# Batch 0 of a windowed attention + SwiGLU kernel in two token halves, with its first q/k as fp32 on a second queue

## The chip, the cores and the metric

The kernel runs on one core of a Trainium2 chip. The metric is device time in microseconds (us), the median of several executions. The engines are named as in the profile: PE (TensorE, matrix products), PEld (PE's weight loads), DVE (VectorE), ACT (ScalarE), POOL (GpSimd), SP (SyncE, which here only issues transfers). "Span" is the length of the profiled execution; the timed runs are some 2 us above it.

## The reference, cut to what matters

```python
# q, k, v: (4, 8, 768, 64) fp32; 8 global keys, local window of 96
scores = scale * (q @ k.T) + bias         # bias = -slope[head] * distance
keep   = is_global | is_local             # keys 0..7, or 0 <= row - col < 96
a      = softmax(where(keep, scores, -1e9))
x      = (a @ v), heads side by side      # (3072 tokens, 512)
g, val = x @ w_gate, x @ w_val            # (512, 1536) each
out    = (silu(g) * val) @ w_out          # (3072, 512) fp32
```

## The kernel before

Tokens are handled in eight blocks of 384, two to a batch; a block has 12 feed-forward steps (gate, value, and one twelfth of the output products of the block before it). "Step 0.2" is block 0, step 2. Attention of later tokens is slipped between the steps. Before the first step can run, batch 0 needs its attention: this **opening** is what the change is about. Attention goes by pairs of heads.

```python
def load_qk(b, h0, h1):                       # POOL's DMA casts fp32 -> fp16
    for st, src in ((qst[b], q), (kst[b], k)):
        nc.gpsimd.dma_start(out=st[:, h0:h1, :], in_=src[b, h0:h1]...)
def load_globals():                           # the 8 global V rows, all batches
    nc.gpsimd.dma_start(out=vG..., in_=v[:, :, 0:NG, :]...)
    for b in range(B):                        # copied in front of all 7 key chunks
        nc.sync.dma_start(out=vSs[b][0:NG, :, :, :], in_=vG[:, b]...broadcast)
# ... issue order of the opening, all on POOL's queue:
load_qk(0, 0, 2); load_globals(); load_v(0, 0); load_v(0, 1)
for hp in range(1, NP): load_pair(0, hp)      # q, k, V of each pair, whole batch
load_w(0); load_w(1); ...
# ... a pair in the opening: all 768 tokens transposed, two of three score banks
#     (exp on ACT, then a multiplication by a mask on DVE), then half the values
def early(hp, s):
    if s == 0:   pairs[0, hp].transposes()
    elif s < 3:  pairs[0, hp].scores(s - 1, nc.vector)
    else:        pairs[0, hp].values(0, True) # num, den; then xT = num / den on DVE
# ... later score banks, values and batch 1's transposes between steps:
single = [[sc(0, 0, 2)], [sc(0, 1, 2)], [va(0, 0, 1)], ..., [tr(1, 0)], ..., [tr(1, 1)]]
```

The softmax here doesn't subtract the row's maximum and nothing guards it: scores larger than these inputs give would overflow.

## Time and profile before

| | before |
|---|---|
| time, median | 264.18 us (263.57 to 264.3) |
| span | 262.0 us |
| step 0.2 starts / step 0.10 starts | 30.25 / 49.48 |
| PE busy / idle in the span | 240.5 / 21.5 |

The prediction below shows the page's busy rows and slices. One more view: the table by stage, cut at first scores, step 0.2, step 0.10, step 1.0, block 2 and block 7. Columns: stretch; its length; busy time (and number of instructions) of PE, PEld, DVE, ACT, POOL; granted clock (of PE, as a share of full speed); DMA share (packet time over that of 16 engines, which can pass 1); GB/s.

```profile
0.00:8.98 8.98, 1.70 (x24) 1.23 (x26) 2.66 (x12) 3.10 (x4) 7.92 (x15) 1.00 0.95 115
8.98:30.25 21.27, 15.64 (x190) 9.74 (x191) 16.55 (x42) 15.25 (x36) 15.86 (x21) 1.00 1.49 183
30.25:49.48 19.23, 17.24 (x210) 10.22 (x210) 18.21 (x44) 9.45 (x20) 9.09 (x12) 1.00 1.41 198
49.48:54.06 4.58, 4.32 (x36) 2.11 (x33) 3.21 (x9) 4.03 (x10) 0.00 (x0) 1.00 1.61 190
54.06:85.69 31.63, 31.63 (x327) 18.58 (x325) 24.95 (x57) 20.65 (x45) 19.39 (x22) 1.00 0.90 86
85.69:226.97 141.28, 138.70 (x1101) 77.80 (x1100) 109.05 (x242) 66.62 (x141) 56.67 (x63) 1.00 0.64 72
226.97:262.00 35.03, 31.31 (x169) 16.34 (x167) 13.91 (x25) 10.07 (x19) 0.00 (x0) 1.00 0.14 53
```

### The profile page before, as it was taken

The page shows a single profiled execution, that of the slowest core. Times are in us where ns is not written, and L with a number is a line of the kernel's source. Part 1 is how long each engine was busy: PE and PEld are TensorE (multiplying, and loading weights), DVE is VectorE, ACT ScalarE, POOL GpSimd, SP SyncE. Part 2 cuts the span into 40 slices and gives each one's busy share as a digit, 9 for nine tenths or more (in the row PEclk, how much of TensorE's full clock was granted, in tenths as well). Part 3 has the DMA queues.
Part 4 walks back from the last instruction along what each step waited for, and adds up shares of the span by engine and source line. Part 5 has one row for each costly group of instructions (what it writes and reads, how often), then busy time and mean ns, then how long its engine had stood idle before and what let it go on. Part 6 is the DMA issues. An engine that isn't in the chain of part 4 may idle for free.

```text
span 262.0 us, 5362 instructions
## 1 busy us (share of the span) xinstructions
PE 240.5 (92%) x2048; PEld 136.0 (52%) x2048; DVE 188.5 (72%) x429; ACT 129.2 (49%) x273; POOL 108.9 (42%) x130
## 2 busy tenths in 40 slices
PE   1685899799999999999999799999999999999994
PEld 0452456455556645545556455555566555555541
DVE  2499799787986898887768987986668655655610
ACT  3668635587656355552653554463743333332321
POOL 8985643205679884184597810202343100000000
PEclk9999999999999999999999999999999999999999
DMA  8999999976699999487999991110100111101122
GB/s 103 167 169 198 191 205 206 175 84 41 77 94 157 124 110 173 63 53 79 144 150 72 144 127 43 40 39 3 41 33 12 43 40 40 40 3 40 43 80 80
DMA packets 79193, 24.41 MB, mean 93 GB/s; under 512 B 66016, under 2 KB 76096, under 8 KB 79168
## 3 DMA queue, kind: packets, MB, share of 16 engines
q0 software_dynamic: 62368, 14.20, 58.9%
q1 hardware_dynamic: 16800, 9.87, 16.1%
q8 instruction: 16, 0.26, 0.4%
q14 instruction: 9, 0.07, 0.1%
HBM read 28.58 MB, written 6.29 MB: 133 GB/s over the span
## 4 chain that ended last, share of the span: by engine, by line
PE 68%; DMA 15%; DVE 8%; ACT 3%; POOL 3%; issue 2%; DVEq 0%; ACTq 0%; POOLq 0%
PE ops L366 22%; PE vps L339 19%; PE gps L339 19%; DMA kst<-in_k_dram 8%; DMA qst<-in_q_dram 4%; DMA wv<-in_moe_w_val_dram 3%; PE den L288 3%; PE scA L253 2%; PE num L288 2%; DVE sl L352 2%; ACT at L259 2%; POOL vS L117 1%; DVE rb L307 1%; DVE dT L301 1%; POOL qst L112 1%
## 5 line engine op out<-in xcount | busy, mean ns | idle before, releaser
L350 ACT ACTIVATE th<-gps 128x384 f32<-128x384 f32 x96 | 47.7, 497 | 79.5 <-PE gps L339 77.1
L339 PE MATMUL vps<-xT,wv 128*128 128x384 f16 x384 | 78.7, 326 | 2.1 <-DVE sl L352 2.0
L339 PE MATMUL gps<-xT,wg 128*128 128x384 f16 x384 | 78.7, 326 | 1.0 <-DVE xT L314 0.5
L352 DVE SCALAR_TENSOR_TENSOR sl<-th,gps 128x384 f32<-128x384 f32 x96 | 52.5, 547 | 34.6 <-ACT th L350 34.1
L366 PE MATMUL ops<-wo,hT 128*128 128x512 f16 x288 | 76.0, 379 | 0.3
L356 DVE TENSOR_TENSOR hT<-vps,sl 128x384 f16<-128x384 f32 x96 | 52.7, 549 | 7.9 <-PE vps L339 0.6
L311 POOL TENSOR_TENSOR xT<-ns,rb 128x384 f16<-128x384 f32 x24 | 24.1, 1005 | 72.9 <-DVE rb L307 64.6
L339 PEld LDWEIGHTS <-wg 128*128 128x128 f16 x384 | 36.3, 98 | 33.3 <-issue 1.9
L339 PEld LDWEIGHTS <-wv 128*128 128x128 f16 x384 | 36.2, 98 | 28.0 <-issue 5.0
L366 PEld LDWEIGHTS <-hT 128*128 128x128 f16 x288 | 27.2, 98 | 25.2 <-issue 1.3
L259 ACT ACTIVATE at<-scA 128x432 f16<-128x432 f32 x48 | 25.7, 536 | 16.3 <-PE scB L253 16.3
L259 ACT ACTIVATE at<-scB 128x432 f16<-128x432 f32 x48 | 25.9, 540 | 0.0
L123 POOL DMA_DIRECT2D vS<-in_v_dram x24 | 21.2, 888 | 4.4 <-DMA wo<-in_moe_w_out_dram 1.7
L371 ACT ACTIVATE osb<-ops 128x512 f32<-128x512 f32 x24 | 14.5, 604 | 15.1 <-PE ops L366 14.8
L270 DVE TENSOR_TENSOR at<-at,masks 128x432 f16<-128x432 f16 x52 | 18.8, 381 | 4.3 <-ACT at L259 3.9
L288 PE MATMUL den<-at,ones 128*64 128x216 f16 (+6 forms) x288 | 17.8, 235 | 3.6 <-DVE at L270 2.0
L307 DVE STREAM_TRANSPOSE rb<-dR 128x384 f32<-128x384 f32 x32 | 18.3, 573 | 1.7 <-DVE dR L302 0.5
L288 PEld LDWEIGHTS <-ones 128*64 128x64 f16 x288 | 11.7, 111 | 13.3 <-issue 10.3
L301 DVE STREAM_TRANSPOSE dT<-den 128x384 f32<-128x384 f32 x32 | 18.3, 570 | 0.4 <-PE den L288 0.3
L322 ACT COPY ns<-num 128x384 f32<-128x384 f32 x24 | 11.5, 481 | 12.5 <-PE num L288 10.8
L253 PE MATMUL scA<-qT,kT 64*128 64x216 f16 (+2 forms) x112 | 14.8, 251 | 2.7 <-DVE kT L219 2.6
L288 PE MATMUL num<-at,vS 128*64 128x216 f16 (+6 forms) x288 | 14.8, 230 | 0.3 <-DVE xT L314 0.3
(36 smaller groups left out, 175.3 us busy)
## 6 DMA issues: line engine op xcount, KB each, us to landing
out_dram<-osb SPq DMA_DIRECT2D x24, 256.0 KB, 2.0
vS<-in_v_dram POOLq DMA_DIRECT2D x20, 120.0 KB, 6.1
wg<-in_moe_w_gate_dram POOLq DMA_DIRECT2D x4, 384.0 KB, 9.3
wv<-in_moe_w_val_dram POOLq DMA_DIRECT2D x4, 384.0 KB, 10.5
wo<-in_moe_w_out_dram POOLq DMA_DIRECT2D x3, 512.0 KB, 14.1
kst<-in_k_dram POOLq DMA_DIRECT2D x16, 96.0 KB, 3.4
qst<-in_q_dram POOLq DMA_DIRECT2D x16, 96.0 KB, 3.5
qst<-in_q_dram POOLq DMA_DIRECT2D x6, 192.0 KB, 5.9
```

What stands on the lines that cost most here:

```text
L123: nc.gpsimd.dma_start(out=vSs[b][NG:NG + n, c, :, :], in_=v[b, :, KC * c:KC * c + n, :].rearrange("h p d -> p h d"))
L253: nc.tensor.matmul(sc[hi][:, col:col + n], lhsT=self.kT[r, 128 * c:128 * c + 128], rhs=self.qT[r, q0:q0 + n], start=True, stop=True)
L259: nc.scalar.activation(out=at, in_=sc[hi][:, 0:BANK], func=AF.Exp, scale=scale)
L288: nc.tensor.matmul(dst[r, o:o + n], lhsT=ones if ones_side else vSs[b][:, c, 2 * hp + hi, :], rhs=self.at[hi, cb][:, col:col + n], start=( ...
L301: nc.vector.transpose(dT[:, 0:n_q], den[:, 0:n_q])
L307: nc.vector.transpose(rb[:, 0:n_q].rearrange("p (n i) -> p n i", i=32), dR[:, 0:nb].unsqueeze(2).broadcast_to([128, nb, 32]))
L311: nc.gpsimd.tensor_mul(dst, ns[:, 0:n_q], rb[:, 0:n_q])
L339: nc.tensor.matmul(gv[f, which][:, 0:TB], lhsT=w[:, c, 128 * f:128 * f + 128], rhs=xT[:, c, TB * t:TB * t + TB], start=(c == 0), stop=(c = ...
L350: nc.scalar.activation(out=th, in_=dst[:, 0:TB], func=AF.Tanh, scale=0.5)
L352: nc.vector.scalar_tensor_tensor(out=sl, in0=th, scalar=1.0, in1=dst[:, 0:TB], op0=AluOp.add, op1=AluOp.mult)
L356: nc.vector.tensor_mul(hTs[t][:, f, :], dst[:, 0:TB], gv["sl"])
L366: nc.tensor.matmul(ops, lhsT=hTs[t][:, f, 128 * i:128 * i + 128], rhs=wo[:, f, :], start=(f == 0), stop=(f == NFF - 1))
```

## The change

The intent: start the feed-forward steps sooner. Batch 0 is cut in two halves of 384 tokens. Only half 0 is done in the opening. Its q/k come as fp32 through SP's queue, which is free, and are cast on DVE and ACT. V comes in chunks of 120 keys. In the opening, and for part of half 1, the distance bias is added by PE (a product of a diagonal matrix with the distances) before the exponential, in place of DVE's mask multiplication. Half 1's attention moves between steps 2 and 9. Steps 0.10 to 1.2 run without output products, which block 1 then makes up ("deferred"). Twelve plus three dummy matmuls are meant to bring PE's clock up.

The diff, cut to its core (smaller changes, such as one mask multiplication for both heads of a pair, are left out):

```diff
+    for hp in range(NP):                      # half 0, fp32, SP's queue
+        for st, src in ((k32, k), (q32, q)):
+            nc.sync.dma_start(out=st[:, 2 * hp:2 * hp + 2, :],
+                in_=src[0, 2 * hp:2 * hp + 2, 0:TB, :].rearrange(
+                    "h (p j) d -> p h (j d)", p=128))
...
-    def load_v(b, h): ...
+    def load_v_first(h0, h1):
+        for c in range(4):
+            n = min(KC, TB - KC * c)
+            nc.gpsimd.dma_start(
+                out=(vS3 if c == 3 else vSs[0][:, c])[NG:NG + n, h0:h1, :],
+                in_=v[0, h0:h1, KC * c:KC * c + n, :].rearrange("h p d -> p h d"))
...
-    WF = 384
+    WF = 256                                  # 6 pairs of weight pieces, not 4
...
+        def bias(self, half, which):          # slopeI = -slope/scale * identity
+            sc = banks("sc")
+            for hi in range(2):
+                for col, d0, n in BIAS[half, which]:
+                    nc.tensor.matmul(sc[hi][:, col:col + n],
+                        lhsT=slopeI[:, 2 * self.hp + hi, :], rhs=dist[:, d0:d0 + n],
+                        start=(col == 0), stop=False, skip_group_check=True)
+            return sc
...
+    load_globals()
+    copy_globals(0)                           # SP, behind the eight q/k loads
+    load_v_first(0, 4)
+    load_v_first(4, 8)
...
+    fill(12)
+    p_cast(0, V, A); p_bias(0); p_tr(0, V); p_cast(1, V, A); fill(3); p_sc(0)
+    p_tr(1, V); p_cast(2, V, A); p_bias(1); p_sc(1)
+    load_w(0); load_w(1); load_w(2)
+    p_va(0); p_tr(2, V); run_later(9); p_cast(3, V, A)
+    load_half(k16[:, 1], k, 1, 0, H); load_half(q16[:, 1], q, 1, 0, H)
+    for c in range(3, NCH): load_v_rest(0, c)
+    load_w(3)
+    for b in range(1, B): copy_globals(b)     # SP
...
+    stretches = [
+        (ff(0, 0, 10), half1),
+        (ff(0, 10, 12) + ff(1, 0, 3), []),    # bare: no output products
+        (ff(1, 3, 12, (1, 1, 2)), fst), ...
```

## The prediction

> **What bounds the kernel now.** I read the page from the top: busy times, then the 40 slices.
>
> ```profile
> PE 240.5 (92%) x2048; PEld 136.0 (52%) x2048; DVE 188.5 (72%) x429; ACT 129.2 (49%) x273; POOL 108.9 (42%) x130
> ...
> PE   1685899799999999999999799999999999999994
> ...
> DVE  2499799787986898887768987986668655655610
> ...
> DMA  8999999976699999487999991110100111101122
> ```
>
> TensorE (PE) has the most work, and a slice is 6.55 us: from the eighth slice on PE is nearly always busy, while in the first seven it is not, and there VectorE (DVE) and the DMA engines stand at 7 to 9. So the kernel has an opening of some 50 us that PE does not set, and then a long stretch that PE does. I cut it at the feed-forward steps, which the timeline shows (block 0 step 2 at 30.25, step 10 at 49.48, block 2 at 85.69):
>
> ```profile
> 0.00:5.79 5.79, 0.00 (x0) 0.00 (x0) 1.38 (x9) 2.30 (x3) 4.74 (x10) 1.00 0.69 102
> 5.79:28.76 22.97, 16.13 (x205) 10.46 (x205) 17.28 (x44) 14.91 (x34) 17.61 (x25) 1.00 1.49 175
> 28.76:49.48 20.72, 18.45 (x220) 10.73 (x220) 18.76 (x45) 10.58 (x22) 10.52 (x13) 1.00 1.40 198
> 49.48:85.69 36.21, 35.95 (x361) 20.68 (x358) 28.16 (x65) 24.68 (x54) 19.39 (x22) 1.00 0.99 99
> 85.69:203.60 117.91, 115.33 (x969) 64.88 (x968) 95.58 (x218) 58.94 (x126) 55.84 (x63) 1.00 0.74 80
> ```
>
> Columns: length, then busy time of PE, its weight loads, DVE, ScalarE (ACT) and GpSimd (POOL), clock, DMA share, GB/s. In 28.76:49.48 DVE is busy 18.8 of 20.7 us: that stretch is DVE's. What ends the opening is also DVE's, the last pair's normalisation:
>
> ```profile
> 28.14 0.56 DVE L314 TENSOR_TENSOR xT<-num,rb 128x384 f16<-128x384 f32 x1
> ...
> 28.76 0.32 PE L339 MATMUL gps<-xT,wg 128*128 128x384 f16 x1 [0.53 <-DVE xT L314]
> ```
>
> The bracket says that PE stood still until DVE had written xT. The waits add two transfers, the first q and batch 1's q:
>
> ```profile
> PE trq L204 <- DMA qst<-in_q_dram: 6.9, 2, 5.8
> PE scA L253 <- DVE kT L219: 2.6, 4, 1.4
> PE den L288 <- DVE at L270: 2.0, 2, 1.0
> ```
>
> Two traps. Overlapping matmuls hide short waits, so I count work instead: in the undisturbed end a feed-forward step (gate, value, a twelfth of the output products) starts every 1.95 us, 0.65 for each of the three. And DVE durations overlap:
>
> ```profile
> 38.27 0.54 DVE L352 SCALAR_TENSOR_TENSOR sl<-th,gps 128x384 f32<-128x384 f32 x1
> 38.73 0.57 DVE L301 STREAM_TRANSPOSE dT<-den 128x384 f32<-128x384 f32 x1
> 39.34 0.23 DVE L302 RECIPROCAL dR<-dT 128x12 f32<-128x12 f32 x1
> 39.48 0.49 DVE L356 TENSOR_TENSOR hT<-vps,sl 128x384 f16<-128x384 f32 x1
> 39.89 0.56 DVE L307 STREAM_TRANSPOSE rb<-dR 128x384 f32<-128x384 f32 x1
> 40.38 0.51 DVE L352 SCALAR_TENSOR_TENSOR sl<-th,gps 128x384 f32<-128x384 f32 x1
> ```
>
> From start to start, sl and hT cost 0.46 and 0.41 to 0.46, so 0.92 a step; a normalisation (dT, dR, rb, xT) costs about 1.8.
>
> **What the Trainium skill says.** "DMA: Bandwidth & Descriptors", section SWDGE vs HWDGE vs iDMA: only GpSimd's DMAs cast. So q/k from the SP queue must land as fp32 and be cast on an engine, as the change does. Its part on issuing engines adds that all queues share the same 16 DMA engines, so a second queue saves only issue time. The trace agrees with the premise: POOL spends 0.7 to 0.9 us on each issue and is busy 17.6 of 23 us in the opening. "TensorE: Matmul & The Clock Gate", Part 1: PE runs at half rate until busy for about 3.4 us. The trace fits: twelve transposes took 0.85 at 5.79 and 0.53 at 19.00. That is what the added dummy matmuls are for. "SBUF — State Buffer", two separate sides: a two-port DVE copy locks GpSimd out of writing descriptors; the new casts are such copies, and no row before shows the cost.
>
> **The change, part by part.**
>
> *First data.* POOL's first q landed at 5.75, k at 6.70. SP issues cost about 0.4 each; the constants (162 KB) landed 2.5 us after issue. Constants, k0, q0 issued at 0.7, 1.1, 1.5 should land by about 4.3. Cast (estimate 0.3 on DVE, 0.5 on ACT), six transposes each, half-width copies (half of 0.9 and 0.8): first scores near 6.4, against 8.98.
>
> *Pairs 0 to 3.* Before, 4.6 to 4.8 us a pair. DVE per pair now: kT copies and globals 0.95, cast 0.3, normalisation 1.8 = 3.05; the two mask products (0.67 + 0.80) are gone. ACT: exps of 432, 432, 168, 168 at about 1.35, qT 0.45, cast 0.45 = 2.25. PE pays 1728 columns of bias a pair over both halves at 0.65/1536 us each, 0.73 us, or 2.9 us in all. Walking the order of instructions with these costs, scores start at 6.4, 8.8, 11.3, 15.35; the last denominators come at 17.5 and the last xT at 20.4 (28.7 before). Block 0 step 2 starts at 22.2, against 30.25: **8 us earlier**.
>
> *But half 1 moves behind it.* Its transposes and kT copies, formerly in the opening, now lie in steps 2 to 9. DVE there, from 21.0: ten steps x 0.92 = 9.2, and per pair kT copies 0.7, one mask 0.55, normalisation 1.8, x4 = 12.2; sum 21.4, so 42.4. PE: eight steps x 1.3 + 7.7 of attention = 18.1, ending at 40.3. DVE is again the bound; with 1 us of unevenness, 43.4. **This gives back about 2 us**: the same point was 49.48 before, less 1.4 for batch 1's first transposes, already done there.
>
> *Transfers.* Saturated, a weight transfer (786 KB read) lands every 1.95 us, 400 GB/s. Half of q/k (1.57 MB), V (0.8) and constants land by about 9.8, the six first weight pieces by 17.6, second q/k halves by 21.5 (needed at 22.2: tight), batch 1's first q/k by about 44, against 49. The 1.6 us of PE waiting for it at 47 to 49.5 should vanish.
>
> *Deferred output products.* No work is removed. Steps 10, 11 and block 1's 0 to 2 run bare: 5 x 1.3 = 6.5, to 49.9. The rest of block 1: nine steps x 1.3, twelve output parts x 0.65, attention 7.8 (four transposes 0.7, score pairs 0.57, values 0.67) = 27.3. Before, by the same count, 3.9 us of 36.2 were lost here; DVE and ACT at some 70% should lose 2. Block 2 starts at 79.2 against 85.69: **6.5 us**.
>
> *After that* the two are nearly the same. Before lost only about 1.7 us in 85.69:203.60 by this count; merged masks and earlier key spreading may save 0.5. Span 262.0 - 6.5 - 0.5 = 255.0; timed runs are about 2.1 above the span, so 257.1. A schedule this finely set has probably been tuned further than my walk allows for, so I take 256.5.
>
> **Rivals.** (1) *DVE swallows the gain*: steps 2 to 9 become so crowded (ACT about 17.6 of 21 us, gate banks three instead of four) that they end at 47 instead of 43.4. For it: DVE's 18.8 of 20.7 already. Then 260 to 261. (2) *Transfers bind*: q/k, V and weights share the same engines, and 256-byte V rows and 1 KB weight rows are small; casts may starve descriptors. V for pair 0 or the second q/k half late by 2 to 3 us gives 259. Against: saturated rows show 400 GB/s, and the opening was limited by issue. (3) *The deferral pays more*: PE work without DVE work now fills block 1, the stalls there and later go to nearly none, and the opening closes at 20: 251 to 253.
>
> **Range and chances.** Faster by 2% means below 258.9. My sum is 2 us under that with an error of perhaps 3.5: 0.75 faster, 0.23 same, 0.02 slower. Slower needs more than 5 us of new stalls, against 8 saved at the start. Range 251 to 261.
>
> **What would show it.** First scores at 6 to 7; last xT of the opening near 20.4; step 2 near 22; DVE at 90% or more until 42 to 44; no PE wait for batch 1's q; block 2 near 79; from there to the end 176 us, as before. The prediction is wrong if step 2 starts after 25, if step 10 starts after 46, or if the part after block 2 changes by over 3 us.

## The result, and the profile after

The changed kernel took **264.91 us** (median of four runs, 264.61 to 265.39), against 263.94 for four runs of the kernel before beside it (the 264.18 above is the median of three of these). The ratio is 1.0038, with a 95% interval of 1.0014 to 1.0063: the same within 2%, and if anything slower. (A ratio here is the mean time of one kernel's fast runs over that of the other's fast runs of the same rounds, so it is not quite the ratio of the medians.)

The busy times and four rows of the slices (6.56 us each) of the changed kernel's page:

```profile
PE 247.5 (94%) x2119; PEld 140.5 (54%) x2119; DVE 183.1 (70%) x420; ACT 134.4 (51%) x295; POOL 102.1 (39%) x119
...
PE   6677999899999999899999999999999999999994
...
PEclk9959999999999999999999999999999999999999
DMA  7999999990146999990158996991011101101122
```

PE's share rose from 92 to 94% of a span that did not shrink: idle time fell by 6.4 us (21.5 to 15.0) and busy time rose by 6.9. By groups of PE's instructions, with overlapping time counted once, the new busy time is 4.9 us of bias products and 3.5 us of dummy matmuls; the rest (transposes, value products, all else) sums to 1.4 less. The clock row shows one slice, the third (13 to 20 us), at half: PE had stood still just before. But the row, and the clock column of the tables by stage, read full speed also where the trace holds no clock record, and here the first record is at 9.80 us. Before it the matmuls' own times say half. The same eight score products:

```profile
7.78 0.68 PE L325 MATMUL sc<-qT,kT 64*128 64x216 f16 x8
20.59 0.43 PE L325 MATMUL sc<-qT,kT 64*128 64x216 f16 x8
```

So by records and times together PE ran at full rate from 9.80 to 13.21 and from 20.04 on; in the kernel before, from 17.32 on.

The table by stage, cut at the same events but for one (step 0.10 at 47.93; then step 1.3, where output products begin again, at 55.92, in place of step 1.0):

```profile
0.00:7.78 7.78, 5.43 (x34) 3.21 (x35) 5.00 (x27) 2.27 (x3) 6.62 (x13) 1.00 0.87 165
7.78:27.15 19.37, 14.28 (x167) 9.74 (x167) 10.02 (x27) 11.16 (x30) 12.12 (x16) 0.82 1.68 190
27.15:47.93 20.78, 20.20 (x251) 11.66 (x248) 17.81 (x45) 15.47 (x40) 10.86 (x14) 1.00 1.43 198
47.93:55.92 7.99, 7.05 (x45) 3.89 (x41) 7.18 (x16) 4.02 (x10) 0.23 (x1) 1.00 1.60 171
55.92:83.75 27.83, 27.83 (x302) 16.14 (x300) 21.17 (x47) 20.02 (x43) 6.53 (x8) 1.00 0.28 34
83.75:227.09 143.34, 141.22 (x1165) 79.58 (x1164) 107.93 (x237) 71.37 (x151) 64.93 (x70) 1.00 0.86 84
227.09:262.50 35.41, 31.47 (x169) 16.32 (x167) 14.01 (x26) 10.06 (x19) 0.83 (x1) 1.00 0.14 52
```

Three things can be read off. Step 0.2 starts at 27.15, 3.1 us earlier than before, not 8. In steps 2 to 9 PE is busy 20.20 of 20.78 us, DVE only 17.81: PE is the fuller engine there, not DVE. And the part after step 0.10 takes 214.6 us, 2.1 *more* than before (262.0 - 49.48 = 212.5).

What held up the opening is in the timeline of PE. In brackets: the idle time before an instruction, and what the profile holds responsible.

```profile
10.36 0.44 PE L325 MATMUL sc<-qT,kT 64*128 64x216 f16 x8
10.72 0.45 PE L396 MATMUL den<-at,ones 128*64 128x216 f16 x8
14.35 0.57 PE L396 MATMUL num<-at,vS 128*64 128x216 f16 x4 [3.18 <-DMA wg<-in_moe_w_gate_dram]
```

The denominators of pair 0 are done at 11.2, the numerators start at 14.35. The name in the bracket is misleading: a numerator does not need a weight of the feed-forward part. The semaphore it waits for is the one of SP's copy of the global V rows. That copy was issued at 7.21, behind SP's eight q/k loads, and the last of its completions came at 14.21. The Trainium skill, "DMA: Bandwidth & Descriptors", section "Why a DMA increments its semaphore by 16 and not by 1", says how to read this: on the hardware queue only the engines that the transfer uses report, one by one, after a first jump, and only the full count means that all has landed. The trace agrees: one jump at 8.49, then eight single updates from 12.28 to 14.21.

The landing times of the trace tell the rest of the opening. "Predicted" are the numbers of the prediction.

| landed (us) | predicted | after |
|---|---|---|
| first q (the first scores need it: predicted 6.4, measured 7.78) | 4.3 | 5.97 |
| V of half 0, last chunk (heads 0-3 / 4-7) | 9.8 | 11.95 / 13.96 |
| sixth weight piece | 17.6 | 24.04 |
| second q/k halves | 21.5 | 26.08 and 28.14 |

The six weight pieces themselves came 1.3 us apart at the end, as the prediction's rate says. But V was 4 us late, and the first weight piece landed only 3 us after V, while SP's copies of the global rows for batches 1 to 3 were running (their last updates: 16.56, 17.91, 18.99).

The longest waits of PE in the changed kernel (total, number, longest):

```profile
PE num L396 <- DMA wg<-in_moe_w_gate_dram: 3.2, 1, 3.2
PE vps L467 <- DVE sl L480: 1.6, 4, 0.7
PE gvps L467 <- DVE xT L424: 1.2, 1, 1.2
...
PE trs L278 <- ACT q L533: 1.2, 1, 1.2
```

The wait for batch 1's q (1.1 of the 6.9 us in the first line of the prediction's list; the other 5.8 are the first q of all) is gone, as predicted, though not for the reason given (see below).

### The profile page after: what moved, and what is told of

It is laid out like the page before. It is cut to its first block, busy times and chain, and to the rows that moved or that the text cites. A ratio compares the mean times of both kernels' runs of the same rounds, so it can differ in the third digit from the quotient of the medians.

```text
span 262.5 us, 5522 instructions
## 1 busy us (share of the span) xinstructions
PE 247.5 (94%) x2119; PEld 140.5 (54%) x2119; DVE 183.1 (70%) x420; ACT 134.4 (51%) x295; POOL 102.1 (39%) x119
## 3 DMA queue, kind: packets, MB, share of 16 engines
q1 hardware_dynamic: 18848, 11.45, 20.2%
## 4 chain that ended last, share of the span: by engine, by line
PE 69%; DVE 16%; ACT 4%; issue 4%; POOL 3%; DMA 2%; POOLq 0%; DVEq 0%; ACTq 0%
PE ops L496 20%; PE vps L467 19%; PE gps L467 18%; PE nd L396 6%; PE sc L348 3%; DVE rb L417 3%; DVE sl L480 3%; DVE dT L412 3%; DMA wg<-in_moe_w_gate_dram 2%; DVE hT L484 2%; POOL vS L154 2%; ACT at L357 2%; DVE xT L424 1%; DVE dR L413 1%; PE trs L252 1%
## 5 line engine op out<-in xcount | busy, mean ns | idle before, releaser
L467 PE MATMUL vps<-xT,wv 128*128 128x384 f16 x376 | 76.7, 326 | 2.0 <-DVE sl L480 1.6
L467 PE MATMUL gps<-xT,wg 128*128 128x384 f16 x376 | 77.0, 327 | 1.3 <-DVE hT L484 0.8
L357 ACT ACTIVATE at<-sc 128x432 f16<-128x432 f32 x72 | 33.0, 538 | 3.7 <-PE sc L348 3.7
L409 ACT COPY ns<-nd 128x384 f32<-128x384 f32 x28 | 13.4, 478 | 17.2 <-PE nd L396 16.4
L417 DVE STREAM_TRANSPOSE rb<-dR 128x384 f32<-128x384 f32 x32 | 18.1, 568 | 0.9
L368 DVE TENSOR_TENSOR at<-at,masks 128x864 f16<-128x864 f16 x20 | 14.4, 721 | 3.4 <-ACT at L357 3.2
L412 DVE STREAM_TRANSPOSE dT<-nd 128x384 f32<-128x384 f32 x28 | 16.1, 573 | 0.3 <-PE nd L396 0.3
L396 PEld LDWEIGHTS <-ones 128*64 128x64 f16 x288 | 11.2, 111 | 7.9 <-issue 7.1
L333 ACT ACTIVATE at<-sc 128x432 f16<-128x432 f32 (+2 forms) x32 | 11.9, 443 | 3.5 <-PE sc L325 3.5
L186 POOL DMA_DIRECT2D kst<-in_k_dram x16 | 13.7, 871 | 0.0
L186 POOL DMA_DIRECT2D qst<-in_q_dram x16 | 13.6, 862 | 0.0
L396 PE MATMUL nd<-at,ones 128*64 128x216 f16 (+6 forms) x256 | 13.2, 231 | 0.0
```

Of the source, the lines that this page charges most:

```text
L186: nc.gpsimd.dma_start(out=st[:, h // 2, :, h % 2, :], in_=src[b, h].rearrange("(t p) d -> p t d", p=128))
L357: nc.scalar.activation(out=at[:, hi, :], in_=sc[hi][:, 0:BANK], func=AF.Exp, scale=scale)
L396: nc.tensor.matmul(dst[r, o:o + n], lhsT=ones[:, 0:64] if ones_side else vals[:, 2 * hp + hi, :], rhs=self.at[cb][:, hi, col:col + n], sta ...
L412: nc.vector.transpose(dT, den[:, 0:TB])
L417: nc.vector.transpose(rb.rearrange("p (n i) -> p n i", i=32), dR.unsqueeze(2).broadcast_to([128, TB // 32, 32]))
L467: nc.tensor.matmul(gv[f, which][:, 0:TB], lhsT=w[:, c, 128 * f:128 * f + 128], rhs=x_of(t)[:, c, :], start=(c == 0), stop=(c == NC - 1))
```

## The experiments

All are edits of the changed kernel, except e8. Each row gives the time, the kernel before in the same rounds, and the ratio; then, from the profiled run, where steps 0.2 and 0.10 start, the span, and "rest" = span less the start of step 0.10. The kernel before falls into two groups in the same rounds, 263.2 to 265.0 and 265.4 to 266.6, and the ratios average over both: against the lower group alone they would be 0.001 to 0.003 higher. The trace of each kernel is of one run. Two kernels, e2 and e12, compute something else.

| run | us | before | ratio (95%) | 0.2 | 0.10 | span | rest |
|---|---|---|---|---|---|---|---|
| before | 263.94 | | | 30.25 | 49.48 | 262.0 | 212.5 |
| after | 264.91 | 263.94 | 1.0038 (1.0014-1.0063) | 27.15 | 47.93 | 262.5 | 214.6 |
| e1 | 269.72 | 264.03 | 1.0208 (1.0168-1.0247) | 24.45 | 52.80 | 267.5 | 214.7 |
| e2 | 265.38 | 264.03 | 1.0046 (1.0008-1.0085) | 28.82 | 49.05 | 263.8 | 214.8 |
| e3 | 264.73 | 264.03 | 1.0012 (0.9952-1.0072) | 27.47 | 48.89 | 263.4 | 214.5 |
| e4 | 268.81 | 264.03 | 1.0164 (1.0121-1.0207) | 25.68 | 52.21 | 266.8 | 214.6 |
| e5 | 264.67 | 264.46 | 0.9999 (0.9953-1.0045) | 27.09 | 47.75 | 262.6 | 214.9 |
| e6 | 265.75 | 264.46 | 1.0044 (1.0000-1.0088) | 27.81 | 48.77 | 263.7 | 214.9 |
| e7 | 265.41 | 264.46 | 1.0026 (0.9981-1.0070) | 27.74 | 48.40 | 263.3 | 214.9 |
| e8 (before, edited) | 264.95 | 264.46 | 1.0006 (0.9952-1.0060) | 30.32 | 48.74 | 263.9 | 215.2 |
| e9 | 267.49 | 264.23 | 1.0103 (1.0051-1.0156) | 25.30 | 50.39 | 265.4 | 215.0 |
| e10 | 263.30 | 264.23 | 0.9960 (0.9922-0.9999) | 24.92 | 46.30 | 261.2 | 214.9 |
| e11 | 264.46 | 264.35 | 0.9987 (0.9939-1.0036) | 24.55 | 46.68 | 262.5 | 215.8 |
| e12 | 262.00 | 264.35 | 0.9903 (0.9865-0.9941) | 23.34 | 45.64 | 260.3 | 214.7 |
| e13 | 262.63 | 264.15 | 0.9920 (0.9878-0.9963) | 24.65 | 45.30 | 260.2 | 214.9 |
| e14 | 262.96 | 264.15 | 0.9936 (0.9888-0.9984) | 24.74 | 44.95 | 260.7 | 215.8 |

The last column already says something: whatever is done to the opening, the rest of the changed kernel takes 214.5 to 215.8 us. The time is decided by when step 0.10 starts.

**Theory A**: the opening and steps 2 to 9 are set by the sum and the order of the transfers, which share the same DMA engines. **Rivals**: PE's new bias products ate the gain; the deferral cost time; DVE is full and gives back whatever the opening gains.

### e1: the first global rows loaded directly

```diff
-    load_globals(); copy_globals(0)
     load_v_first(0, 4)
+    first_globals()   # four POOL loads: v[0, :, 0:8] into chunks 0, 1, 2 and the cut one
     load_v_first(4, 8)
+    load_globals(); copy_globals(0)      # SP's copy, now for chunks 3 and up only
```

> The changed kernel's PE stands still 3.2 us (11.2 to 14.35) before its first num product. Theory A: what it waits for is not a weight load, as the wait row says, but the copy of the 8 global V rows, which sits on the SP queue behind the eight fp32 q/k loads and lands at 14.21. With these rows loaded straight from DRAM by GpSimd (four loads of 64 rows), num should start near 12 to 12.5, the half-rate clock after the stall should go, and block 0 step 2 should start at 24 to 25 instead of 27.15. The end then moves by 2 to 3 us to about 262 us if nothing later absorbs it. Rival B: the second q/k halves (landing 26.1 and 28.1) and the crowded steps 2 to 9 absorb it: step 10 stays within 1 us of 47.9 and the time stays at 264 to 265.

Step 0.2 came 2.7 us earlier, at 24.45, so the copy had held it up. But the kernel got slower by 4.8 us. Its longest waits of PE:

```profile
PE trs L281 <- DMA k<-in_k_dram: 2.9, 1, 2.9
PE trs L281 <- DMA q<-in_q_dram: 2.4, 1, 2.4
```

The second q/k halves landed at 28.07 and 30.81. SP's copies now ran while the weights came, and these landed 2.4 to 2.7 us apart in place of 1.3 (17.49, 19.88, 22.62, 25.21). The Trainium skill, "DMA: Bandwidth & Descriptors", section "Queues, rings and completion order", has each DMA engine take turns between the queues that have work for it. The landing times fit that: a small copy on one queue slowed large loads on the other. A wait was taken away and a longer one came in its place. The clock added to it: by its records PE was at half rate from 29.08 to 35.90, after these waits, and its busy time between steps 0.2 and 0.10 was 22.53 us in place of 20.20.

### e2: no bias products (wrong)

```diff
-            for hi in range(2):
-                for col, d0, n in BIAS[half, which]: nc.tensor.matmul(...)
...
-                        rhs=self.qT[r, q0:q0 + n], start=not biased, stop=True,
+                        rhs=self.qT[r, q0:q0 + n], start=True, stop=True,
```

> Wrong on purpose: the bias products of batch 0 (40 matmuls) are left out and nothing replaces them. Theory A (waits for transfers and DVE set the opening): step 2 moves by less than 0.5 us, since PE is idle there anyway; steps 2 to 9 get shorter by 4 x 0.3 = 1.2 us of PE work; the time falls by about 1 us, to 264. Rival C (PE work added by the change is what ate the gain): the whole estimate of 2.9 us comes back, 262 us.

All 40 bias products are gone, the relative error is 0.45, and the time is 265.38, which neither theory had. Steps 2 to 10 became 0.55 us shorter (20.23), and step 0.2 came 1.7 us later. Of that, 1.1 are SP's copy of the global rows, which landed at 15.32 in place of 14.21. And PE stayed at half rate until 25.70 (eight score products still took 0.68 at 21.90). So leaving the bias out did not bring the gain back; but as the clock changed with it, e2 does not show what the bias costs in the opening by itself.

### e3: no deferral

```diff
-        (ff(0, 10, 12) + ff(1, 0, 3), []),
-        (ff(1, 3, 12, (1, 1, 2)), fst),
+        (ff(0, 10, 12), []),
+        (ff(1, 0, 12, (1,)), fst),
```

> The output products of block 0 are not put off: block 1 has one part per step and attention of batch 1 from its step 0. My prediction gave the bare steps a use. Theory A: the deferral moves PE work without removing any and gains nothing by itself, but it gives the loads of batch 1's q/k (landing 48.9 to 54.7) time: without it PE waits for them at about 51 and the time is 1 to 2 us longer, 266 to 267. Rival D: the five bare steps (8.0 us measured for 6.5 of PE work) are themselves a loss that the deferral causes; without it the time falls by 1 us or more, to 263 to 264.

From step 0.10 to block 2 it takes 35.99 us against 35.82 with the deferral, and the rest 214.5 against 214.6. Both A and D missed: the deferral is worth nothing and costs nothing that these runs could show.

### e4: first q/k halves through POOL, as fp16

```diff
-        for st, src in ((k32, k), (q32, q)): nc.sync.dma_start(...)      # and no casts
+    load_first(0); load_globals(); copy_globals(0); load_first(1)         # POOL, casting
+    load_v_first(0, 4); load_first(2); load_first(3); load_v_first(4, 8)
```

> The fp32 SP loads and the casts are undone: q/k of batch 0's first half come as fp16 from GpSimd, in token halves as in the changed kernel, pairs 0 and 1 ahead of V. Theory A (all loads share the same engines and their sum sets the opening): the first scores come within 1 us of 7.8 and step 2 within 1.5 us of 27.15, and the time is 264 to 266. Rival E (the SP queue is what brought the first data forward): first scores at 9 to 10, step 2 at 29 or later, time 266 to 268.

This undoes the second queue. The first scores start *earlier* than with it, at 6.21 against 7.78, which neither A nor E had, and so does step 0.2 (25.68 against 27.15). So the queue of its own did not bring the first data forward. Step 0.2 is not the queue's work alone, though: with SP free, the copy of the global rows was issued at 6.02 and landed at 9.66, not at 14.21. Then the second halves land at 27.59 and 29.69, PE waits 1.1 and 1.7 us for them, runs at half rate from 29.03 to 35.86, and the kernel is 1.6% slower than the one before. It is e1's pattern again.

### e5, e6, e7: the copies late, V whole, the halves first

```diff
 # e5: copies for batches 1 to 3 by POOL, at steps 0.9 and 1.2, not by SP in the opening
-    for b in range(1, B): copy_globals(b)
+    at_step(0, 9, ..., lambda: copy_globals(1))
+    at_step(1, 2, lambda: copy_globals(2), lambda: copy_globals(3))
 # e6: e5, and first_globals() as in e1, but behind V of all heads
+    load_v_first(0, 8); first_globals(); load_globals()
 # e7: e6, and the third pair of weight pieces behind the second q/k halves
-    load_w(2)
     load_half(k16[:, 1], k, 1, 0, H); load_half(q16[:, 1], q, 1, 0, H)
+    load_w(2)
```

> One thing alone: the copies of the global V rows of batches 1 to 3 leave the SP queue (where they run at 12 to 19 us) and go to GpSimd behind batch 1's q/k. Batch 0's copy stays. In the run with direct globals the weight pieces landed 2.4 to 2.7 us apart while these copies ran and 1.3 us apart before and after. Theory A (the sum of what must land before the second q/k half sets the opening, and these small copies are a costly part of it): the second q half lands 2 to 3 us before 28.14, with step 2 still near 27 because batch 0's copy is unchanged, steps 2 to 4 keep near 4.8, the time 263 to 265. Rival F (the copies ride along for nothing, the weight loads were slow for another reason): the second q half stays at 27.5 to 28.5.

The weights now land 1.3 to 1.6 us apart from 15.02 on, and the second halves 2 us earlier, at 24.02 and 26.17: SP's copies had cost that. But PE still waits for batch 0's copy (2.0 us) and step 0.2 does not move (27.09), so the earlier halves are worth nothing.

> Both mended: copies late, batch 0's first global rows straight from DRAM, V of the first half in 4 loads of all heads instead of 8, so that GpSimd issues less. Theory A: num of pair 0 starts at about 12 to 13, step 2 at 24 to 25 as in the run with direct globals, and the second q half lands at 25 to 26, so that steps 2 to 4 wait about 1 us, not 5; step 10 at 45 to 46, the time 261.5 to 263.5. Rival B (steps 2 to 9 absorb): step 10 at 47 or later, time 264.

> As the last, and the second q/k halves are loaded ahead of the third pair of weight pieces, which is needed two steps later. Theory A: the second q half lands 2.6 us earlier (23 or before), step 2 at 24 to 25 and no wait for it, step 4 by 30, step 10 at 44 to 45.5, the time 260.5 to 262.5, faster than both kernels. Rival B: step 10 at 47 or later, time 264, since DVE and PE need 20 us for steps 2 to 9 with queues between them however early they start.

Both missed. The global rows now came behind V of all heads and landed, for the first chunk, at 14.45 and 14.20. By its semaphores pair 0's first numerator waited for these, and PE stood for 2.7 and 3.1 us: step 0.2 at 27.8 and 27.7. (In e6 and e7 alike the profile names another load.) In e9 below the same rows, loaded between the two parts of V, landed at 11.46. So what pair 0 needs must not stand behind V of the other heads. In part it may be chance: in e6, 15 of the 16 completions of V's third chunk were in at 11.89, the last only at 13.89.

### e8: the same for the kernel before

```diff
 # before: copies for batches 1 to 3 by POOL, behind load_qk(1, 2, 4) and V of batch 1
-        for b in range(B): nc.sync.dma_start(out=vSs[b][0:NG], ...)
+        copy_globals(0, nc.sync)
...
+    copy_globals(1, nc.gpsimd); ...; copy_globals(2, nc.gpsimd); copy_globals(3, nc.gpsimd)
```

> The kernel before with the same one mend: copies of batches 1 to 3 out of the opening. If the copies cost the transfers 1.3 us each as theory A has it, the third and fourth pairs' q/k there land 2 to 4 us earlier (they landed at 15.3 and 18.9), but DVE at 4.6 us a pair was as much its bound: the last xT comes 0 to 2 us before 28.7, the time is 262 to 264. Rival F: nothing moves.

Pairs 2 and 3 had their k at 14.06 and 17.61 in place of 15.26 and 18.92, and step 0.2 came at 30.32 as ever. The opening of the kernel before is not set by these transfers. Step 0.10 did come 0.7 us earlier, but then PE waited 2.0 us for batch 1's q and k of the third pair, which landed at 56.00 and 57.96 in place of 54.21 and 56.15. "Copies late" is not a gain in itself.

### e9 and e10: e1 and e5 together; then the halves first

```diff
 # e9: order of e1, copies late as in e5 (batch 0's behind load_w(3))
+    load_v_first(0, 4); first_globals(); load_v_first(4, 8); load_globals()
 # e10: e9, and load_w(2) behind the second q/k halves
```

> Wrong theory or right: e1 (global rows of the first chunks loaded directly, between the V loads of heads 0-3 and 4-7) brought step 2 forward to 24.45 but its other copies, still on SP, slowed the weights and the second q/k halves (28.07/30.81). Here the order of e1 is kept and all copies that are not needed in the opening are issued late by GpSimd, as in e5. Theory A (the opening is a sum and order of transfers: each of e1 and e5 took away one of two limits, only both together pay): step 2 at 24.2-25, second q/k halves landed by 24.0 and 26.2, wait of PE for them under 0.5, steps 2 to 10 in 20.5-21.5, step 10 at 45.0-46.3, the rest 214.7, span 259.7-261, time 262-263.3, ratio to before 0.990-0.995. Rival B (the gain is eaten by VectorE and PE in steps 2-9 whenever the opening ends earlier): steps 2 to 10 in 23 or more with no wait for q or k, time 264.5 or more. Rival C (the second halves cannot land before 26 whatever): PE waits 1-2 for them, step 10 at 47, time 264.

> As e9, with the third pair of weight pieces moved behind the second q/k halves, which so need to wait for four pieces and not six. Theory A: the second halves land 2.6 earlier than in e9 (about 21.5 and 23.6), the third pair of weight pieces at about 24.5 and 26, needed only by step 4 at about 29; so no wait for q or k at all, step 10 at 44.8-46, time 262-263.2: as e9 or up to 0.5 less. Rival C (it is the halves that bind in e9): clearly less than e9, by 0.5-1.5. Rival B: as e9, at 264.5 or more.

e9 missed: the weights landed 1.3 to 1.7 us apart from 17.45 on, so the halves came at 26.81 and 29.07, and PE waited 0.7 us for k and 1.9 for q. Rival C came nearest. Its clock was at half too, from 30.36 to 33.77 (PE busy 21.86 us between steps 0.2 and 0.10). e10, which only swaps two pairs of transfers, took these waits away: step 0.2 at 24.92, 0.10 at 46.30, and 263.30 us. Here three edits stand together, the direct rows, the late copies and the halves ahead (not every pair of them was run), and the last swap alone is worth 4.2 us between e9 and e10, waits and clock together.

### e11 and e12: what still sets the two parts?

```diff
 # e11: e10, half 1's first scores masked by DVE again, not biased by PE
-            p.scores_half(1, which, banks("sc") if which else p.bias(1, 0), not which)
+            p.scores_half(1, which, banks("sc"), False)
 # e12: e10, q/k of pairs 2 and 3 not loaded (casts read pairs 0 and 1): wrong on purpose
-    for hp in range(NP):
+    for hp in range(2):
```

> What sets steps 2 to 9 (21.4 from step 2 to step 10 in e10)? This is e10 with the first scores of half 1 masked by VectorE multiplications again (two for each pair, some 0.5 a pair) in place of TensorE's bias matmuls (16 in all, some 1.6). Theory A (TensorE is the bound there: 20.2 of 20.8 busy in the changed kernel, VectorE 17.8): steps 2 to 10 in 19.6-20.6, step 10 about 1 earlier than in e10, the rest unchanged at 214.7, time 262.0-262.8. The prediction's view (VectorE is the bound): steps 2 to 10 in 22.5 or more, time 264.3 or more. Rival C (neither, a chain through both): within 0.4 of e10.

> Wrong on purpose: e10 with the first q/k halves of pairs 2 and 3 not loaded at all (their casts read pairs 0 and 1 again), which takes 0.79 MB out of the opening and no instruction of any engine but four issues on SP. Theory A (the bytes moved set the opening): V, weights and second q/k halves land some 2 earlier, step 2 at 22.5-23.3 instead of 24.9, steps 2 to 10 as in e10, time 261-262. Rival (a chain of casts, copies, exps and normalisations of four pairs sets the opening by now): step 2 at 24.4-25, time 263 as e10.

e12: without 0.79 MB of the opening's reads, step 0.2 comes 1.6 us earlier (23.34). Bytes count there, for most of the 2.0 that they would take at the rate of the weight pieces (524 KB in 1.33 us), an estimate. (The clock differs too: e12 is at full rate from 10.27 on, e10 is at half from 8.07 to 14.89.) (Its output passed the tolerance, though about an eighth of all tokens has wrong scores in half of its heads.) But step 0.10 gains only 0.7: from 0.2 to 0.10 it now takes 22.30. e11 took 22.13 there, and decided nothing, because PE waited 0.7 us for q and 0.9 for a copy of global rows that I had put too late.

### e13 and e14: those waits taken away

```diff
 # e13: e10 with
-    load_half(k16[:, 1], k, 1, 0, H); load_half(q16[:, 1], q, 1, 0, H)
-    load_w(2)
+    load_half(k16[:, 1, 0:4], k, 1, 0, 4); load_half(q16[:, 1, 0:4], q, 1, 0, 4)
+    load_w(2); copy_globals(0)           # no longer behind load_w(3)
+    load_half(k16[:, 1, 4:], k, 1, 4, H); load_half(q16[:, 1, 4:], q, 1, 4, H)
 # e14: e13, and half 1's first scores masked by DVE as in e11
```

> This is e10 with two late transfers mended: the second q/k halves of heads 0 to 3 go alone ahead of the third pair of weight pieces (their q lands about 2 earlier, near 23.7), those of heads 4 to 7 behind it, and the copy of batch 0's global rows for the later chunks is issued before these (it landed at 34.8 and TensorE waited 0.5 for it). Theory A (in e9 to e12 the stretch from step 2 to 10 grew above 20.8 only by waits for transfers): step 2 at 24.5-25, steps 2 to 10 in 20.5-20.9, step 10 at 45.2-45.8, rest 214.8, span 260.2-260.7, time 262.2-262.9. Rival (VectorE takes it back): steps 2 to 10 stay at 21.3 or more with no wait for a transfer, time 263.3 or more.

> e13 with e11's masks: half 1's first scores masked by VectorE, not by TensorE's bias products. Without the waits for transfers that e11 had (0.7 and 0.9), the stretch from step 2 to 10 tells which engine sets it. TensorE sets it: 16 matmuls (0.39 a pair, 1.6) less, so about 1 less than e13, 19.5-20, time 0.8 less than e13. VectorE sets it: VectorE has 1.1 more work (19.0 against 17.8), so 0.5 or more longer than e13. A chain through both: within 0.3 of e13.

The tables by stage, cut at steps 0.2, 0.10 and 1.3; first e13:

```profile
0.00:24.65 24.65, 17.94 (x200) 11.61 (x201) 14.50 (x54) 13.45 (x33) 19.02 (x30) 1.00 1.23 165
24.65:45.30 20.65, 20.07 (x249) 11.62 (x247) 17.80 (x45) 15.45 (x40) 12.88 (x18) 1.00 1.53 194
45.30:53.30 8.00, 7.05 (x45) 3.90 (x42) 7.19 (x16) 4.03 (x10) 2.99 (x4) 1.00 1.30 203
```

then e14:

```profile
24.74:44.95 20.21, 19.40 (x235) 10.52 (x232) 18.87 (x51) 15.39 (x40) 12.20 (x17) 1.00 1.53 194
44.95:53.42 8.47, 7.04 (x44) 3.90 (x41) 7.63 (x17) 4.03 (x10) 3.31 (x4) 1.00 1.31 204
```

e13 did what theory A said: steps 2 to 10 are back to 20.65, and between 24 and 46 us only one wait of PE of over 0.2 us is left (0.6, for a kT copy of DVE). At 262.63 us it **beats both kernels**, the one before by 0.8% (0.9920, interval 0.9878 to 0.9963; by 0.5% against its lower group, and each of e13's six runs is below each of the 11 beside it). The changed kernel was not run in these rounds. So the 0.7 us that e10 lost between steps 2 and 10 came from late transfers, and DVE took nothing back; what e11 and e12 lost beyond that was not tested apart.

e14 then moves 0.7 us of busy time from PE and puts 1.1 on DVE. Steps 2 to 10 get *shorter*, by 0.44, not longer: DVE is not the bound there, though the prediction said so. But the gain is smaller than the work removed, and the bare steps after it get longer by 0.47 (PE's wait for DVE's sl there grows from 0.7 to 1.2), so it is gone at step 1.3. None of the three expected cases came as stated: PE weighs more than DVE in steps 2 to 9, but DVE is close behind.

One rival was not in the list: the clock. The changed kernel was at half rate from 13.21 to 20.04, e13 from 9.66 on at full rate. But e14, at half from 11.06 to 17.88, starts step 0.2 only 0.1 later than e13. So the clock is not what e13 gained in the opening.

## Why the prediction was wrong

The working came to a span of 255.0; it was 262.5. By its own steps:

| step of the sum | predicted | measured | error |
|---|---|---|---|
| step 0.2 starts | 22.2 | 27.15 | +4.95 |
| steps 0.2 to 0.10 | 21.2 | 20.78 | -0.4 |
| step 0.10 to the end | 211.6 | 214.6 | +3.0 |

The other 0.9 us to the 256.5 are the 0.6 that I took off without a reason from a view, and 0.3 between the span of the profiled run and the median. Of the three signs that the prediction named for being wrong, two came: step 2 after 25 and step 10 after 46. The part after block 2 changed by 2.4, less than its 3.

**Failed: "should land by about 4.3" and "landed by about 9.8".** The rate of 400 GB/s was read from weight transfers in a saturated stretch. From 3.79 to 13.96, worked out from the sizes, some 2.2 MB of q, k and V were read, 220 GB/s. The walk through the opening then took PE's, DVE's and ACT's durations and let V be there. Rival (2) named the case ("V for pair 0 or the second q/k half late by 2 to 3 us gives 259"), but I counted only one of the two, and did not see the copies of the global rows in the diff: they moved behind eight loads on the queue that the change had filled. A better order, with the first global rows loaded directly, recovers 2.5 of the 4.95 (e13 against the changed kernel, step 0.2 at 24.65). Of the 2.45 left, bytes are a part (e12), and the chain of casts, copies and normalisations is presumably the other; the runs do not divide it.

**Failed: "from there to the end 176 us, as before".** I compared the start of block 2 in both, but not how much attention was done by then. Counted from the trace: before had 440 attention matmuls left at that point, the changed kernel has 504. The part after block 2 took 178.75 us against 176.31, and PE's busy time in it rose by 2.7. So the predicted "6.5 us" at block 2 was not like for like. What the kernel really had in hand at step 0.10 was 1.55 us, and of that 1.4 were two pairs of batch 1's transposes that it had not yet done.

**Failed: the deferral.** "3.9 us of 36.2 were lost here" was set against the profile's own row, which the prediction shows: PE 35.95 busy of 36.21. Most of the 3.9 was work that my count had left out (the 64 matmuls). e3 measured the deferral at nothing. The bare steps took 8.0, not 6.5, and the rest of block 1 took 27.8, not 29.3: the two errors cancel.

**Half right: "DVE is again the bound" and "gives back about 2 us".** The length was right (21.2 against 20.78). The reason was not: DVE was busy 17.8 us of it, where the walk summed 21.4 from start to start; PE was busy 20.2, where the walk had 18.1. The views said so before: the prediction's row 28.76:49.48 has PE at 18.45 beside DVE's 18.76, and of the seven slices in which it calls PE not busy, the sixth and seventh (33 to 46 us) show PE at 9. e14 agrees: more work for DVE did not lengthen these steps.

**Right, but by luck**: PE no longer waits for batch 1's q. The reason was wrong: its first q and k were to land by about 44 and landed at 50.84 and 48.91, no earlier than the ones waited for before (47.91 and 48.98); PE no longer waits because the first transposes moved to 57.31. **Right**: the casts cost about what was said (ACT 0.51 to 0.55, DVE 0.35 to 0.63); whether they held up POOL's descriptors, as rival (2) feared, no run shows apart. Bias was sized at 2.9 and measured at 4.9 (4.2 in e13, which had more of it at full clock), but without it, in e2, the time did not fall.

A plain budget would have warned of this. PE was busy for 240.5 us before. With the 2.9 of bias that the prediction counted and the dummies (3.5 as measured) it is 246.9, which leaves 8.1 us of idle time in a span of 255.0. Outside the opening the kernel before already idled 8.6, and only 2.0 of that, between steps 0.2 and 0.10, lay where the change could reach it. So the prediction asked for an opening that idles 1.5 us or little more. The changed kernel's idles 7.4, e13's 6.7.

## What to carry to other kernels

Before trusting a walk through the instructions, subtract: the span you predict, less the bounding engine's work, is the idle time that you claim will be left; see in which rows it could be. When an opening waits for data, list every transfer with its size and its place on its queue, small copies too, and ask of each which instruction needs it; moving one limit alone (e1, e4, e5) gave a new wait or nothing, and so did two (e9); taking away all that bound paid. And compare two schedules only at points where the same work has been done.

## What the Trainium skill lacked or had wrong

- "DMA: Bandwidth & Descriptors", "Queues, rings and completion order": it says that engines take turns between queues, but not what a small transfer on one queue costs large ones on the other. Here: weight pieces landed 2.4 to 2.7 us apart while SP's copies of the global rows ran (e1), and 1.3 to 1.7 apart in the same order without them (e9); in e5 two late q/k loads came 2 us earlier once these copies were moved.
- "DMA: Bandwidth & Descriptors", "Issuing engine by pattern": it calls the hardware queue generally faster, and has no figure for a load that needs a cast as well. Here (fp32 in DRAM, needed as fp16) the first scores came at 6.21 with POOL's casting loads (e4) and at 7.78 with SP's fp32 loads and casts; the order of the loads differed as well, so no run shows the queue alone.
- "TensorE: Matmul & The Clock Gate", Part 1: its table has the clock fall to half after at least one idle window of about 3.4 us. (Elsewhere the page knows of falls from shorter idle times, but it gives no busy share of the window at which they come.) Here it fell without an idle window. In the 16 traces, up to 36 us and in the 3.41 us windows of their clock records, PE was busy for 10 to 66% of the window before each of the 12 falls; its longest stop in such a window was 0.5 to 2.5 us. In e10 the clock fell at 8.07 after a window with PE busy for 61%. Windows that kept full rate had 52% and more. All 28 rises came after windows with PE busy for 89% or more, which agrees with the page's busy window.
- No page says that a profile may put a wait down to the wrong transfer. Here it named a weight load for 3.2 us that belonged to a copy of V's global rows; the times of the semaphore's updates showed it.
